# The last, half-empty contraction block of a SwiGLU down projection, run as pairs of 64-row matmuls

## The chip, the cores and the metric

The kernel runs on one core of one Trainium2 chip. The metric is the device time of one execution in microseconds (us). The engines are named as the profile names them: PE does matmuls, PEld loads their stationary operand, DVE is the vector engine, ACT the scalar engine, POOL the general one, and SP issues nearly all DMAs.

## The reference

One adaLN block on 2048 tokens of width 640: a spectral filter (layer norm, 2-D FFT, a filter, inverse FFT) and a SwiGLU feed-forward, each with scale, shift and gate from a small conditioning vector. Only the feed-forward matters here; its inner width is 1728.

```python
def _B_ref(x, w_gate, w_up, w_down):          # x (1, 2048, 640), F = 1728
    g = _silu(x @ w_gate)
    u = x @ w_up
    return g * u @ w_down
...
sa, ca, ga, sb, cb, gb = (mod[:, 0].copy(), ...)
x = x + ga * _A_ref(h, A_w_r, A_w_i)
h = _layernorm(x, axis=-1) * (1 + cb) + sb
x = x + gb * _B_ref(h, B_w_gate, B_w_up, B_w_down)
```

## The kernel before

The whole program is written out by hand: each engine does its instructions in the order of the source, and the tile framework adds the semaphore waits. The first part (up to about 97 us of the span) is the spectral filter. It ends in the loop over `dinv`, which leaves the new residual `x1` in SBUF.

The feed-forward takes the 2048 tokens in four chunks of 512 (`sc`), and each chunk as four tiles of 128 tokens (`tl`). The inner width 1728 is 13 blocks of 128 and one of 64; `NFC` is 14, and block 13 is the half-full one.

For one chunk PE first computes gate and up of block 13 together (`gu13`, L727: 64 gate columns and 64 up columns side by side in `Wp13`). ACT applies Silu to the gate half and copies the up half. A DMA on SP (`u13b`, L734) brings the up half to partitions 0 to 63, and DVE multiplies the two into `AT[0:64, 13, :]` after block 2 (L746). Then, for each of the 13 full blocks, PE computes `gps` and `ups` (L740, five matmuls of 512 columns each), ACT takes Silu of `gps` (L743), and DVE multiplies into `AT[:, fc, :]` (L744). `AT` is double-buffered over the chunks (`ATa`, `ATb`). Between these steps DVE and SP prepare the layer norm of the next chunk: `ln2_stats`, `ln2_newton`, `ln2_xn`, the DMA transpose `ln2_turn` (L649), and `ln2_affine` on DVE and ACT.

The down projection (L767 to L777) follows. For each token tile and each half of the 640 outputs (`oa`, `ob`), 14 matmuls of 320 columns accumulate over the blocks: stationary `AT[:, fc, tok]`, moving `Wd_sb[:, fc, half]`. Block 13 is done like the others with 128 rows: rows 64 to 127 of it are zeros in `AT` (L718) and in `Wd_sb` (L600), set once by POOL. DVE adds the residual out of PSUM (L776), and SP stores the tile (L777).

`Wd_sb` arrives by two DMAs (L599 for 13 blocks, L601 for the 64 rows of the last), ahead of `Wu` (L607) and `wm_gb` (L609) in SP's queue. In chunk 0, DVE multiplies the gate `gb` into the 14 blocks of `Wd_sb` (L753), a few after each block of the loop (`folds`); blocks 11, 12 and 13 come after the last.

PSUM is full: the tags `va`, `vb`, `oa` and `ob` have two buffers each. `gu13` and `gps` take `va`, `ups` takes `vb`, and the down projection takes `oa` and `ob`.

Earlier in the program there are a few matmuls on a part of the array: L369 (one row), L536 (one column) and the transpose in `gate_turn` (L256, five columns).

Of the kernel before, what the change touches and what calls it, by code (L numbers as in the profile page):

```python
# [10 lines left out]
F32 = mybir.dt.float32  # L11
BF16 = mybir.dt.bfloat16
ACT = mybir.ActivationFunctionType
ALU = mybir.AluOpType
AX = mybir.AxisListType

S, D, FF = 2048, 640, 1728
NT, P = 16, 128
# [6 lines left out]
NFC = 14  # L25
# [110 lines left out]
def adaln_block_kernel(  # L136
# [12 lines left out]
    nc = tc.nc  # L149
# [8 lines left out]
    out_v = out.rearrange("o (p t) d -> p (o t) d", t=NT)  # L158
# [13 lines left out]
    g_bc = [const.tile([P, D], BF16, name=n) for n in ("ga_bc", "gb_bc")]  # L172
# [254 lines left out]
    with tc.tile_pool(name="ph2", bufs=2) as ph2, \  # L427
# [122 lines left out]
        for it in range(NU + 2):  # L550
            if it == 0:
                PPs[0] = [product(0, h, X) for h, X in enumerate(Xs.pop(0))]
            if it + 1 < NU:
                Xs[it + 1] = stage_a(it + 1)
            if it + 2 < NPE:
                t2(it + 2)
            if it == 0:
                mod_shat(0, 128)
            if 0 < it < NU:
                X = Xs.pop(it)  # L560
                PPs[it] = [product(it, 0, X[0])]
            if 0 <= it - 1 < NU:
                PP = PPs.pop(it - 1)
                Y2s[it - 1] = []
                for h in range(len(PP)):
                    yps = stage_b(it - 1, h, PP[h])
                    Y2s[it - 1].append(evict_y(it - 1, h, yps))
            if 0 < it < NU and len(X) > 1:
                PPs[it].append(product(it, 1, X[1]))
            if it == 1:  # L570
                m_ps = ps2.tile([P, 2, NC5], F32, name="m_ps", tag="eps_", bufs=2)
                mod_cols(m_ps[:, 0], wm_g, 0)
                mod_cols(m_ps[:, 1], wm_g, 1)
                nc.scalar.copy(g_col[0][:], m_ps[:, 0])
                nc.scalar.copy(modcols[:, 3, :], m_ps[:, 1])
                nc.scalar.add(one_p_cb[:], m_ps[:, 1], 1.0)
                gate_turn(ps2, "eps_", 2, 0)
                nc.sync.dma_start(wm_sb[:], wm_v[:, :, 3 * D:4 * D])
                nc.sync.dma_start(Rinv_sb[:], Rinv_dram)
                gate_spread(0)  # L580
            if 0 <= it - 2 < NU:
                stage_c(it - 2, Y2s.pop(it - 2))
            if 4 <= it < 8:
                epx(it - 4)
            if it in (8, 9):
                nc.vector.tensor_tensor(Rinv_sb[:, it - 8], Rinv_sb[:, it - 8],
                                        g_bc[0][:, it - 8::2].unsqueeze(1).to_broadcast([P, 3, 320]), ALU.mult)
            if it == 5:
                transposed(6)
                transposed(7)  # L590
                nc.sync.dma_start(Htab[:], H_dram)
            if it == 6:
                Wg = big.tile([P, NC5, FFM], BF16, name="Wg", tag="wg")
                nc.sync.dma_start(Wg[:], B_w_gate[:, 0:FFM].rearrange("(c5 dp) f -> dp c5 f", dp=P))
                for i, w_ in enumerate((B_w_gate, B_w_up)):
                    nc.sync.dma_start(Wp13[:, :, 64 * i:64 * i + 64], w_[:, FFM:FF].rearrange("(c5 dp) f -> dp c5 f", dp=P))  # L596
            if it == 8:
                Wd_sb = big.tile([P, NFC, D], BF16, name="Wd_sb", tag="b21a")
                nc.sync.dma_start(Wd_sb[:, 0:13, :], B_w_down[0:FFM, :].rearrange("(fc fp) d -> fp fc d", fp=P))  # L599
                nc.gpsimd.memset(Wd_sb[64:128, 13, :], 0.0)  # L600
                nc.sync.dma_start(Wd_sb[0:64, 13, :], B_w_down[FFM:FF, :])  # L601
            if it == NU + 1:
                m_ps = ps2.tile([P, NC5], F32, name="m_ps", tag="xps", bufs=2)
                mod_cols(m_ps, wm_sb, 0)
                nc.scalar.copy(modcols[:, 2, :], m_ps[:])
                Wu = big.tile([P, NC5, FFM], BF16, name="Wu", tag="wu")
                nc.sync.dma_start(Wu[:], B_w_up[:, 0:FFM].rearrange("(c5 dp) f -> dp c5 f", dp=P))  # L607
                wm_gb = big.tile([P, NC5, D], BF16, name="wm_gb", tag="wb")
                nc.sync.dma_start(wm_gb[:], wm_v[:, :, 5 * D:6 * D])  # L609
# [4 lines left out]
    x1 = x_sb  # L614
# [38 lines left out]
    def ln2_affine(sc, c5s):  # L653
        h2T = h2T_all[:, sc % 2]
        for c5 in c5s:
            if c5 % 2 == 0:
                nc.vector.tensor_scalar(h2T[:, :, c5, :], h2T[:, :, c5, :], one_p_cb[:, c5:c5 + 1], modcols[:, 2, c5:c5 + 1],
                                        ALU.mult, ALU.add)
            else:
                nc.scalar.activation(h2T[:, :, c5, :], h2T[:, :, c5, :], ACT.Identity,  # L660
                                     scale=one_p_cb[:, c5:c5 + 1], bias=modcols[:, 2, c5:c5 + 1])
# [52 lines left out]
    mod_cols(mg_ps, wm_gb, 0)  # L714
    nc.scalar.copy(g_col[1][:], mg_ps[:])
    AT2 = [big.tile([P, NFC, 512], BF16, name=n, tag=g) for n, g in (("ATa", "wb"), ("ATb", "b35"))]
    for a in AT2:
        nc.gpsimd.memset(a[64:128, 13, :], 0.0)  # L718
    nc.scalar.activation(warm[:], rstd2[:, 3:4], ACT.Silu)

    folds = {5: (0,), 6: (1,), 7: (2,), 8: (3, 4), 9: (5, 6), 10: (7, 8), 11: (9, 10), 12: (11, 12, 13)}
    for sc in range(4):
        h2T = h2T_all[:, sc % 2]
        AT = AT2[sc % 2]
        gu13 = ps3.tile([P, 512], F32, name="gu13", tag="va")
        for c5 in range(NC5):
            nc.tensor.matmul(gu13[:], lhsT=Wp13[:, c5, :], rhs=h2T[:, :, c5, :],  # L727
                             start=(c5 == 0), stop=(c5 == NC5 - 1))
        sg13 = ph4.tile([64, 512], F32, name="sg13", bufs=1)
        nc.scalar.activation(sg13[:], gu13[0:64, :], ACT.Silu)  # L730
        u13 = ph4.tile([P, 512], BF16, name="u13", bufs=1)
        nc.scalar.copy(u13[64:128, :], gu13[64:128, :])
        u13b = ph4.tile([64, 512], BF16, name="u13b", bufs=1)
        nc.sync.dma_start(u13b[:], u13[64:128, :])  # L734
        for fc in range(NFC - 1):
            gps = ps3.tile([P, 512], F32, name="gps", tag="va")
            ups = ps3.tile([P, 512], F32, name="ups", tag="vb")
            for w_, o in ((Wg, gps), (Wu, ups)):
                for c5 in range(NC5):
                    nc.tensor.matmul(o[:], lhsT=w_[:, c5, fc * 128:(fc + 1) * 128], rhs=h2T[:, :, c5, :],  # L740
                                     start=(c5 == 0), stop=(c5 == NC5 - 1))
            sg = ph4.tile([P, 512], F32, name="sg", bufs=2)
            nc.scalar.activation(sg[:], gps[:], ACT.Silu)  # L743
            nc.vector.tensor_tensor(AT[:, fc, :], ups[:], sg[:], ALU.mult)  # L744
            if fc == 2:
                nc.vector.tensor_tensor(AT[0:64, 13, :], u13b[:], sg13[:], ALU.mult)  # L746
            if sc == 0:
                if fc == 0:
                    gate_turn(ps3, "oa", 2, 1)
                    gate_spread(1)  # L750
                for f in folds.get(fc, ()):
                    n = P if f < 13 else 64
                    nc.vector.tensor_tensor(Wd_sb[0:n, f, :], Wd_sb[0:n, f, :], g_bc[1][0:n, :], ALU.mult)  # L753
            if sc < 3:
                n0 = 4 * (sc + 1)
                if fc in (1, 2, 3, 4):
                    ln2_stats(n0 + fc - 1)
                if fc == 5:
                    ln2_newton(sc + 1)
                if fc in (6, 7):  # L760
                    ln2_xn(n0 + 2 * (fc - 6))
                    ln2_xn(n0 + 2 * (fc - 6) + 1)
                if fc == 7:
                    ln2_turn(sc + 1)
        if sc < 3:
            ln2_affine(sc + 1, range(NC5))
        for tl in range(4):  # L767
            t = 4 * sc + tl
            tok = slice(tl * 128, (tl + 1) * 128)
            xo = ph4.tile([P, D], BF16, name="xo", bufs=3)  # L770
            os_ = [ps3.tile([P, 320], F32, name=n) for n in ("oa", "ob")]
            for h in range(2):
                for fc in range(NFC):
                    nc.tensor.matmul(os_[h][:], lhsT=AT[:, fc, tok], rhs=Wd_sb[:, fc, h * 320:(h + 1) * 320],  # L774
                                     start=(fc == 0), stop=(fc == NFC - 1))
                nc.vector.tensor_tensor(xo[:, h * 320:(h + 1) * 320], os_[h][:], x1[:, t, h * 320:(h + 1) * 320], ALU.add)  # L776
            nc.sync.dma_start(out_v[:, t, :], xo[:])  # L777


@with_exitstack  # L780
# [45 lines left out]
```

## Time and profile before

| what | us |
|---|---|
| median of 3 runs | 281.56 (280.31 to 281.94) |
| the profiled execution: span, first to last instruction | 279.0 |
| the profiled execution: whole time | not given beside its span; the median lies 2.56 above it |
| PE busy in the span | 268.6 (96%) |
| DVE busy | 163.6 (59%) |
| ACT busy | 112.8 (40%) |
| matmuls of gate and up, L740 (520) | 129.2 |
| matmuls of the down projection, L774 (448) | 66.3 |
| DVE adds of the output, L776 (32) | 15.7 |

The page shows one execution. Busy time of PE adds up the stretches in which at least one matmul is in flight; the mean length of a matmul (299 ns for 320 columns) is longer than its step in a stream, since neighbours overlap. Weight loads (PEld) run beside matmuls. A line of the timeline gives the start, the length, the engine, the source line, the operation with output and inputs, its tile (rows*columns), the moving shape, the count, and in brackets how long the engine stood idle before it and for whom. The granted clock is full in every slice.

### The profile page before, as it was taken

The numbers are of one execution on the slowest core, as the hardware profiler recorded it, in microseconds if no ns is written. First come the engines' busy times: TensorE is split into PE (matmuls) and PEld (weight loads), VectorE is DVE, ScalarE is ACT, GpSimd is POOL, SyncE is SP. The second block draws the span as 40 slices with busy tenths as digits, with TensorE's granted clock in tenths as the row PEclk, the third lists the DMA queues.
The fourth block names the chain that finished last, engine by engine and source line by source line (L and its number), as shares of the span: only waits on it lengthen the run. The fifth ranks groups of instructions, "written<-read, shape, count | busy, mean of one in ns | idle before, by whom it ended". The sixth has DMA issues, their size and how long they took to land.

```text
span 279.0 us, 5262 instructions
## 1 busy us (share of the span) xinstructions
PE 268.6 (96%) x2120; PEld 170.3 (61%) x2120; DVE 163.6 (59%) x411; ACT 112.8 (40%) x220; POOL 10.5 (4%) x34
## 2 busy tenths in 40 slices
PE   6899979999899999999999999999999999999995
PEld 6567768998787844446754445764444774444673
DVE  4999966799499738876227845224872422422322
ACT  5998666998455663222022323003233103223000
POOL 1000023312000010000000000000000000000000
PEclk9999999999999999999999999999999999999999
DMA  7989999999994100050110050101013011000011
GB/s 263 411 220 209 349 324 183 220 307 366 356 363 77 29 27 6 0 96 0 49 56 3 0 96 0 47 26 33 0 33 63 25 47 35 1 0 2 0 47 47
DMA packets 40634, 30.82 MB, mean 110 GB/s; under 512 B 29281, under 2 KB 37410, under 8 KB 40482
## 3 DMA queue, kind: packets, MB, share of 16 engines
q1 hardware_dynamic: 40608, 30.49, 38.3%
q8 instruction: 16, 0.26, 0.4%
q14 instruction: 8, 0.07, 0.1%
q10 hardware_dynamic: 2, 0.00, 0.0%
HBM read 22.88 MB, written 3.93 MB: 96 GB/s over the span
## 4 chain that ended last, share of the span: by engine, by line
PE 74%; DMA 10%; SPq 9%; DVE 4%; ACT 1%; issue 1%; ACTq 0%; DVEq 0%
PE gps L740 20%; PE ups L740 20%; PE ob L774 11%; PE oa L774 10%; DMA Wd_sb<-in_B_w_down_dram 4%; SPq L218 4%; DMA wm_sa<-in_w_mod_dram 3%; DMA Gtab<-tab_G 2%; PE oa L689 2%; SPq L596 2%; PE gu L727 2%; PE ob L689 1%; DVE x_sb L692 1%; SPq L223 1%; PE yps L488 1%; PE xps L463 1%
## 5 line engine op out<-in xcount | busy, mean ns | idle before, releaser
L740 PE MATMUL gps<-h2T_all,Wg 128*128 128x512 bf16 x260 | 64.6, 379 | 0.0
L740 PE MATMUL ups<-h2T_all,Wu 128*128 128x512 bf16 x260 | 64.6, 379 | 0.0
L743 ACT ACTIVATE sg<-gps 128x512 f32<-128x512 f32 x52 | 31.0, 597 | 74.0 <-PE gps L740 72.3
L740 PEld LDWEIGHTS <-Wu 128*128 128x128 bf16 x260 | 25.5, 98 | 30.6
L740 PEld LDWEIGHTS <-Wg 128*128 128x128 bf16 x260 | 25.4, 98 | 30.5
L744 DVE TENSOR_TENSOR ATb<-ups,sg 128x512 bf16<-128x512 f32 x26 | 17.9, 690 | 32.0 <-PE ups L740 32.0
L744 DVE TENSOR_TENSOR ATa<-ups,sg 128x512 bf16<-128x512 f32 x26 | 17.9, 687 | 20.4 <-PE ups L740 17.5
L774 PEld LDWEIGHTS <-ATa 128*128 128x128 bf16 x224 | 21.9, 98 | 9.3 <-issue 0.5
L774 PEld LDWEIGHTS <-ATb 128*128 128x128 bf16 x224 | 21.9, 98 | 8.8
L730 ACT ACTIVATE sg<-gu 64x512 f32<-64x512 f32 x4 | 2.3, 586 | 46.6 <-PE gu L727 46.6
L776 DVE TENSOR_TENSOR xo<-ob,x_sb 128x320 bf16<-128x320 f32 x16 | 7.9, 492 | 22.1 <-PE ob L774 22.1
L776 DVE TENSOR_TENSOR xo<-oa,x_sb 128x320 bf16<-128x320 f32 x16 | 7.8, 491 | 18.4 <-PE oa L774 18.4
L774 PE MATMUL oa<-Wd_sb,ATa 128*128 128x320 bf16 x112 | 16.8, 299 | 0.1
L774 PE MATMUL oa<-Wd_sb,ATb 128*128 128x320 bf16 x112 | 16.5, 299 | 0.0
L774 PE MATMUL ob<-Wd_sb,ATb 128*128 128x320 bf16 x112 | 16.5, 299 | 0.0
L774 PE MATMUL ob<-Wd_sb,ATa 128*128 128x320 bf16 x112 | 16.5, 299 | 0.0
L309 PE MATMUL zps<-Rs,hT 128*128 128x328 bf16 x90 | 14.7, 303 | 0.1
L280 DVE BATCH_NORM_STATS2 st<-x_sb 128x6 f32<-128x320 bf16 x32 | 13.8, 470 | 0.8 <-DMA x_sb<-in_A_x_dram 0.8
L681 ACT CAST VT<-va 128x512 bf16<-128x512 f32 x16 | 9.4, 586 | 8.0 <-PE va L677 6.2
L488 PE MATMUL yps<-identb,PP 128*128 128x128 bf16 x162 | 11.5, 219 | 0.6 <-DVE PP L479 0.4
L466 ACT CAST X<-xps 128x512 bf16<-128x512 f32 (+1 forms) x21 | 11.2, 598 | 1.6 <-PE xps L464 1.6
L309 PEld LDWEIGHTS <-hT 128*128 128x128 bf16 x96 | 8.8, 98 | 4.8 <-ACT hT L305 0.8
(204 smaller groups left out, 407.0 us busy)
## 6 DMA issues: line engine op xcount, KB each, us to landing
out_dram<-xo SPq DMA_DIRECT2D x16, 160.0 KB, 1.8
Wg<-in_B_w_gate_dram SPq DMA_DIRECT2D x1, 2080.0 KB, 12.8
Wd_sb<-in_B_w_down_dram SPq DMA_DIRECT2D x1, 2080.0 KB, 13.4
Wu<-in_B_w_up_dram SPq DMA_DIRECT2D x1, 2080.0 KB, 9.7
x_sb<-in_A_x_dram SPq DMA_DIRECT2D x3, 640.0 KB, 9.3
wm_g<-in_w_mod_dram SPq DMA_DIRECT2D x2, 800.0 KB
Gtab<-tab_G SPq DMA_DIRECT2D x4, 384.0 KB, 8.2
Htab<-tab_H SPq DMA_DIRECT2D x1, 1536.0 KB, 7.1
```

Of the source, the lines that this page charges most:

```text
L218: nc.sync.dma_start(to[0:15, 0], wv[1:16, 0])
L280: nc.vector.bn_stats(sts[t][:, h, :], x_sb[:, t, 320 * h:320 * h + 320])
L309: nc.tensor.matmul(zap, lhsT=hTs[t][:, 2 * r + i, :], rhs=Rs[:, 3 * r + i, :], start=(i == 0), stop=(i == 2))
L466: nc.scalar.copy(X[:, :n].rearrange("p i c k j -> p i (c k j)"), xps[:, :n, :])
L488: nc.tensor.matmul(yps[:, i, :], lhsT=PP[:, i, cp].rearrange("p a k j -> p (a k j)"), rhs=identb[:], start=(cp == 0), stop=(cp == 1))
L681: nc.scalar.copy(VTs[t][:, 0:4, :], va[:])
L689: nc.tensor.matmul(os_[odd][:], lhsT=VT[:, 2 * odd + ci if ci < 2 else 4, :], rhs=Rinv_sb[:, odd, ci, :], start=(ci == 0), stop=(ci == 2))
L740: nc.tensor.matmul(o[:], lhsT=w_[:, c5, fc * 128:(fc + 1) * 128], rhs=h2T[:, :, c5, :], start=(c5 == 0), stop=(c5 == NC5 - 1))
L743: nc.scalar.activation(sg[:], gps[:], ACT.Silu)
L744: nc.vector.tensor_tensor(AT[:, fc, :], ups[:], sg[:], ALU.mult)
L774: nc.tensor.matmul(os_[h][:], lhsT=AT[:, fc, tok], rhs=Wd_sb[:, fc, h * 320:(h + 1) * 320], start=(fc == 0), stop=(fc == NFC - 1))
L776: nc.vector.tensor_tensor(xo[:, h * 320:(h + 1) * 320], os_[h][:], x1[:, t, h * 320:(h + 1) * 320], ALU.add)
```

## The change

Block 13 is no longer padded with zeros. Its 64 rows, of `Wd_sb` and of `AT`, are held twice, on partitions 0 to 63 and 64 to 127. A second DMA brings the weight rows, and a DMA from SBUF to SBUF copies the rows of `AT` in each chunk. The three memsets on POOL go. The fold of the gate into block 13 covers all 128 rows.

For block 13 the output half `h = 0` uses rows 0 to 63 and `h = 1` rows 64 to 127, so that a token tile has a pair of 64-row matmuls in place of two of 128 rows. The eight of a chunk stand together, after the 13 full blocks of the first two tiles and before those of the last two. For the first two tiles they end the accumulation, for the last two they start it. Since all four tiles are then open at once, the last two accumulate in the tags `va` and `vb`. The output adds of the first two tiles come after the group.

```diff
-                nc.gpsimd.memset(Wd_sb[64:128, 13, :], 0.0)
-                nc.sync.dma_start(Wd_sb[0:64, 13, :], B_w_down[FFM:FF, :])
+                for o in (0, 64):
+                    nc.sync.dma_start(Wd_sb[o:o + 64, 13, :], B_w_down[FFM:FF, :])
...
-    for a in AT2:
-        nc.gpsimd.memset(a[64:128, 13, :], 0.0)
...
                 nc.vector.tensor_tensor(AT[0:64, 13, :], u13b[:], sg13[:], ALU.mult)
+                nc.sync.dma_start(AT[64:128, 13, :], AT[0:64, 13, :])
...
-                    n = P if f < 13 else 64
-                    nc.vector.tensor_tensor(Wd_sb[0:n, f, :], Wd_sb[0:n, f, :], g_bc[1][0:n, :], ALU.mult)
+                    nc.vector.tensor_tensor(Wd_sb[:, f, :], Wd_sb[:, f, :], g_bc[1][:], ALU.mult)
...
+        acc = [[ps3.tile([P, 320], F32, name=("oa", "ob")[h], tag=(("oa", "ob"), ("va", "vb"))[tl // 2][h])
+                for h in range(2)] for tl in range(4)]
+
+        def down13(tl, h):
+            r = slice(64 * h, 64 * h + 64)
+            nc.tensor.matmul(acc[tl][h][:], lhsT=AT[r, 13, tl * 128:(tl + 1) * 128],
+                             rhs=Wd_sb[r, 13, h * 320:(h + 1) * 320], start=(tl > 1), stop=(tl < 2))
+
+        def down(tl, h):
+            for fc in range(NFC - 1):
+                nc.tensor.matmul(acc[tl][h][:], lhsT=AT[:, fc, tl * 128:(tl + 1) * 128],
+                                 rhs=Wd_sb[:, fc, h * 320:(h + 1) * 320],
+                                 start=(tl < 2 and fc == 0), stop=(tl > 1 and fc == NFC - 2))
...
+        for tl in range(2):
+            for h in range(2):
+                down(tl, h)
         for tl in range(4):
-            t = 4 * sc + tl
-            tok = slice(tl * 128, (tl + 1) * 128)
-            xo = ph4.tile([P, D], BF16, name="xo", bufs=3)
-            os_ = [ps3.tile([P, 320], F32, name=n) for n in ("oa", "ob")]
             for h in range(2):
-                for fc in range(NFC):
-                    nc.tensor.matmul(os_[h][:], lhsT=AT[:, fc, tok], rhs=Wd_sb[:, fc, h * 320:(h + 1) * 320],
-                                     start=(fc == 0), stop=(fc == NFC - 1))
-                nc.vector.tensor_tensor(xo[:, h * 320:(h + 1) * 320], os_[h][:], x1[:, t, h * 320:(h + 1) * 320], ALU.add)
-            nc.sync.dma_start(out_v[:, t, :], xo[:])
+                down13(tl, h)
+        for tl in range(2):
+            for h in range(2):
+                x_out(tl, h)
+        for tl in range(2, 4):
+            for h in range(2):
+                down(tl, h)
+                x_out(tl, h)
```

`x_out(tl, h)` is the add of the residual for one half, with the store of the tile after the second half.

## The prediction

> **What bounds the kernel now.** I read the page first: busy time, the forty slices, and the chain that ended last.
>
> ```profile
> PE 268.6 (96%) x2120; PEld 170.3 (61%) x2120; DVE 163.6 (59%) x411; ACT 112.8 (40%) x220; POOL 10.5 (4%) x34
> ...
> PE   6899979999899999999999999999999999999995
> ...
> PE 74%; DMA 10%; SPq 9%; DVE 4%; ACT 1%; issue 1%; ACTq 0%; DVEq 0%
> ```
>
> The matmul engine is busy in 96% of the span, and from slice 15 (about 98 us) on every slice shows 9 but the last, which holds the closing add and store. The change lies wholly in that stretch, the feed-forward part. Next I read the chain in order of time around the end of the first chunk.
>
> ```profile
> 137.00 1.90 PE ob L774 x14
> 138.90 1.90 PE oa L774 x14
> 140.80 1.90 PE ob L774 x14
> 142.71 1.08 PE gu L727 x5
> ```
>
> Fourteen matmuls of 320 columns take 1.90 us, so one takes 0.136 us of the stream (the 299 ns that the groups give is latency, and neighbours overlap). The next group starts when the last one ends: nothing but PE sets the time, so every nanosecond of PE stream saved here comes off the end, and every one added goes on it. The one exception is the first chunk:
>
> ```profile
> 126.89 2.51 PE L774 MATMUL oa<-Wd_sb,ATa 128*128 128x320 bf16 x14
> 127.16 0.69 DVE L744 TENSOR_TENSOR ATa<-ups,sg 128x512 bf16<-128x512 f32 x1 [0.67 <-PE ups L740]
> 127.77 1.28 DVE L753 TENSOR_TENSOR Wd_sb<-Wd_sb,gb_bc 128x640 bf16<-128x640 bf16 x3
> 128.70 0.10 PEld L774 LDWEIGHTS <-ATa 128*128 128x128 bf16 x1 [0.22 <-issue]
> ...
> 129.10 0.37 PEld L774 LDWEIGHTS <-ATa 128*128 128x128 bf16 x3 [0.30 <-issue]
> 129.23 0.43 PE L774 MATMUL ob<-Wd_sb,ATa 128*128 128x320 bf16 x2
> ```
>
> The first 14 matmuls need 126.89 to 129.23 = 2.34 us where 1.90 is the rule. Two loads stand waiting, at 128.70 and 129.10: DVE is still folding the gate into weight blocks 11, 12 and 13 (three operations from 127.77 to 129.05).
>
> Last, how PE passes between a full array and a tile of it. The built program marks three kinds of matmul before as partial tiles (32 rows at L369; 32 columns at L536 and L256); here they are in the timeline of PE.
>
> ```profile
> 2.12 0.29 PE L369 MATMUL cps<-one,c_row 1*128 1x1 bf16 x5 [2.12 <-DMA c_row<-in_c_dram]
> 2.35 1.46 PE L267 MATMUL w_ps<-identb 128*128 128x128 bf16 x12
> ...
> 42.89 0.28 PE L446 MATMUL t2ps<-identb,A_sb 128*128 128x128 bf16 x2
> 43.09 0.82 PE L536 MATMUL sps<-Rp,sa_col 128*1 128x256 bf16 x6
> 43.94 0.23 PE L463 MATMUL xps<-Ktab,B 128*128 128x128 bf16 x1
> ...
> 45.07 1.37 PE L243 MATMUL m_ps<-sc_col,wm_g 128*128 128x1 bf16 x49
> ...
> 99.65 1.24 PE L740 MATMUL ups<-h2T_all,Wu 128*128 128x512 bf16 x5
> 100.83 0.22 PE L256 MATMUL gT_ps<-identb,gb_col 128*5 128x128 bf16 x1
> 100.98 1.25 PE L740 MATMUL gps<-h2T_all,Wg 128*128 128x512 bf16 x5
> ```
>
> Into the tile: five ups matmuls at 0.216 end their stream at 100.73, the small tile starts at 100.83: 0.10 us. Out: its 128 columns take 0.055 (the step of neighbouring 128-column matmuls), and the next starts at 100.98: 0.095. Before L536, two steps of 0.055 from 42.89 give 43.00 and the start is 43.09: 0.09. After it, 6 x 0.109 give 43.745 and the start is 43.94: 0.20, but there the load waited for ScalarE too. After L369, the only row tile, five steps of 0.032 give 2.28 and the next starts at 2.35: 0.07. So a switch costs 0.07 to 0.20, and I take 0.095, where the row nearest in place (L256, inside this stage) stands.
>
> **The change, part by part.**
> - *Removed:* 8 of the 112 matmuls of a chunk (the blocks fc = 13 of four tiles by two halves), 8 x 0.136 = 1.088 us.
> - *Added:* 8 matmuls of 64 rows, as four pairs on rows 0 to 63 and 64 to 127. The built program gives the two members different tile positions (0 and 64), and they write different PSUM tiles (oa and ob, or va and vb). If the members run side by side, four pairs take 4 x 0.136 = 0.544, plus a lag of the last member of about 0.03 (one issue: the 49 loads and matmuls at 45.07 need (1.37 - 0.16) / 48 = 0.025 each). No row shows two row tiles at once, so this is bounded: 0.544 if fully parallel, 1.088 if not at all. I take parallel, since the members differ in rows, in PSUM tile and in position, and nothing in the program orders one behind the other.
> - *Two switches per chunk,* 2 x 0.095 = 0.19 (0 to 0.40). So the group takes 0.544 + 0.03 + 0.19 = 0.764 and saves 0.324 per chunk, **1.30 us over four**.
> - The TensorE page of the Trainium skill ("TensorE: Matmul & The Clock Gate", Measured speedup vs the span model) has four row tiles at 3.07 times one, 77% of the full gain. By that share two tiles would give 1.53, the eight matmuls 0.71 and the change in all -1.0 us, 280.5; this is an estimate, and no run here shows it yet.
> - *The stall in the first chunk.* Block 13 is now needed only after both first tiles, 52 matmuls on. Block 12 still holds its matmul to about 128.70; the next would then start at 128.84, not at 129.10. **0.26 us saved, once.** What is late next is nothing on DVE: its affine steps merely follow.
> - *The copy of AT's block 13 to rows 64 to 127* (SP, 64 KB, four times). Its twin u13b takes 0.48 us to issue and lands in 1.9 us. In chunk 0, DVE ends that block at 106.9, so it lands near 109.3; the group comes near 134. It waits on SP for DVE; queued behind it is only the transpose of the next chunk, which itself waits for DVE several steps later (SP waits 18.4 us there). Zero; if the cover went it would cost about 2 us a chunk.
> - *A second copy of the last weight rows* (80 KB) ahead of Wu and wm_gb. The present one took 4.20 us to issue at 66.75, Wu 0.38 at 73.78. If the new one takes 4.2 too, Wu and wm_gb are issued up to 1.3 us later; they land about 83.5 and 85.4 now and are first read at 99.4 and 96.7. Zero, 11 us of cover.
> - *Three POOL memsets* (0.5 to 0.6 us each) go, off the path. The fold of block 13 covers 128 rows instead of 64: 477 to 484 ns for all fourteen, so zero.
> - *Evictions.* Four adds of 0.49 us now come in one burst (2.0 us) beside the 26 matmuls of the third tile (3.5 us). Tiles three and four sit in va and vb, whose last users (the Silu of fc 12 ends 0.6 us after its matmuls) are 7 us past. The next chunk takes the third tile's buffers first; the fourth tile's first half is evicted during its second half (1.77 us). The last add and output DMA stay as they are. Zero.
>
> Sum: -1.30 - 0.26 = -1.56 us. The profiled execution spans 279.0; the median of the runs shown, 281.56, lies 2.56 above it, and the page gives no time of its own for that execution beyond the span. That surround is untouched: span 277.5, time **280.0**.
>
> **Rivals.** A: the forecast. With switches of 0 to 0.20 it gives -2.44 to -0.72, so 279.1 to 280.8.
>
> B: the pairs run side by side, but a load for a row half waits until the matmul in that half has ended. Then three of four pairs expose a load, at most the 0.095 of a switch: 0.764 + 0.285 = 1.05 per chunk, -0.16 - 0.26 = -0.42, 281.1. Against it: at full size loads of 98 ns hide wholly under 0.136 us matmuls on the same rows. The same TensorE page (Part 3, The mechanism) says that a load overlaps matmuls in flight only when the row group differs; by that rule B holds. The 98 ns loads hidden here differ from it, at full size at least.
>
> C: the change does not do what it says: the members run one after the other with loads hidden. 1.088 + 0.19 = 1.278, +0.76 - 0.26 = +0.50, 282.1.
>
> D, slower: one after the other, and in the 64-row mode each load stands exposed. At 0.095 for seven loads the group takes 1.94 us, +3.42 - 0.26 = +3.16, **284.7**. It turns past +1.41 us when a load shows more than 0.033 us, since 4 x (0.19 + 7 x 0.033) - 0.26 = 1.4. For it: no row shows a pair running together, and the only row tiles (L369) step at 0.032 where full ones step at 0.025. Against it: the 32-column tiles of L536 step at 0.109 for 256 columns, loads hidden.
>
> **How the numbers follow.** About 0.5% (1.41 us) is what a measurement of this kernel can tell from no change. A has 0.62: 0.48 beyond that bound, 0.14 short of it (larger switches). B has 0.12 and C 0.08, both within it; D 0.18. So faster 0.48, same 0.34, slower 0.18. The range holds A, B and C: 279.1 to 282.1, each end moved out by 0.3, since the three runs themselves lie 280.31 to 281.94; that is 278.8 to 282.4, and D is left out. A's own range is 279.1 to 280.8.
>
> **What would show it.** In the trace after: the 64-row matmuls of a pair starting within 0.03 us of each other and the next pair 0.136 later (A); a step of up to 0.23 between pairs (B); eight steps of 0.136 (C) or more (D). From the last matmul of the second tile to the first of the third: 0.76 us in A. The first 14-matmul stretch of chunk 0 short by 0.26. The prediction is wrong if this group takes over 1.09 us, or if a new wait of PE shows up at it or at the start of a chunk.

## The result and the profile after

The changed kernel takes 279.06 us in the median of 8 runs (278.70 to 280.41), the kernel before 280.89 in 8 runs beside it. The ratio is 0.9942, with a 95% interval of 0.992 to 0.9964. The profiled execution took 279.14 us, with a span of 277.4; that of before had a span of 279.0.

From the page of the changed kernel, busy time and the chain that ended last:

```profile
PE 267.5 (96%) x2120; PEld 168.3 (61%) x2120; DVE 162.6 (59%) x411; ACT 112.7 (41%) x220; POOL 8.9 (3%) x31
...
PE 86%; DVE 7%; DMA 2%; ACT 2%; issue 1%; SPq 0%; ACTq 0%; DVEq 0%
```

PE is still the bound. Its busy time falls by 1.1 us and the span by 1.6; of the difference, 0.5 lies in the first 40 us, which the edits do not touch (35.7 us busy before, 36.2 now). So the gain is read from starts, first in the chain in order of time. Before:

```profile
97.64 1.10 PE gu L727 x5
...
187.06 1.08 PE gu L727 x5
...
275.80 0.49 DVE xo L776
```

And in the changed kernel:

```profile
97.54 1.10 PE gu L725 x5
...
140.25 1.77 PE ob L775 x13
142.01 1.08 PE gu L725 x5
...
186.03 1.08 PE gu L725 x5
...
274.11 0.49 DVE xo L785
```

From one chunk's `gu13` to the next it is now 186.03 - 142.01 = 44.02 us; before it was 187.06 - 142.71 = 44.35. Each chunk after the first is 0.33 us shorter. The first, from 97.54 here and 97.64 before, has 44.47 in place of 45.07, 0.60 shorter. The timeline of the changed kernel shows both reasons, the start of chunk 0's down projection and its group of pairs:

```profile
126.79 2.11 PE L775 MATMUL oa<-Wd_sb,ATa 128*128 128x320 bf16 x13
127.67 1.28 DVE L751 TENSOR_TENSOR Wd_sb<-Wd_sb,gb_bc 128x640 bf16<-128x640 bf16 x3
128.60 1.05 PEld L775 LDWEIGHTS <-ATa 128*128 128x128 bf16 x8 [0.22 <-issue]
128.74 1.11 PE L775 MATMUL ob<-Wd_sb,ATa 128*128 128x320 bf16 x7
...
132.94 1.25 PE L775 MATMUL ob<-Wd_sb,ATa 128*128 128x320 bf16 x8
134.12 0.39 PEld L770 LDWEIGHTS <-ATa 64*128 64x128 bf16 x8 [0.26 <-issue]
134.13 0.31 PE L770 MATMUL oa<-Wd_sb,ATa 64*128 64x320 bf16 x1
134.13 0.31 PE L770 MATMUL ob<-Wd_sb,ATa 64*128 64x320 bf16 x1
134.27 0.30 PE L770 MATMUL oa<-Wd_sb,ATa 64*128 64x320 bf16 x1
...
134.54 0.30 PE L770 MATMUL oa<-Wd_sb,ATa 64*128 64x320 bf16 x1
...
134.78 0.99 PE L775 MATMUL oa<-Wd_sb,ATa 128*128 128x320 bf16 x6
```

One load waits instead of two: the first 13 matmuls take 128.74 - 126.79 = 1.95 us, 0.18 over their 1.77, where before 14 took 0.44 over 1.90. A stream is taken to end one step (0.136 us) after its last start. The eight full matmuls from 132.94 end their stream at 134.03, and the first pair starts at 134.13, both members within 0.01 us; the next pair follows at 134.27. The last pair starts at 134.54 and ends its stream at 134.68; the full tile goes on at 134.78. The group takes 0.75 us, two switches of 0.10 us included.

On SP, the two weight copies and what was queued behind them:

```profile
68.00 4.09 SPq L601 DMA_DIRECT2D Wd_sb<-in_B_w_down_dram  x2
73.67 0.38 SPq L607 DMA_DIRECT2D Wu<-in_B_w_up_dram  x1
```

Both copies together took 4.09 us to issue, from 68.00 to 72.09, and `Wu` went out at 73.67 (73.78 before).

### The profile page after: what moved, and what is told of

The parts are those of the page before. It is cut to its first block, busy times and chain, and to the rows that moved or that the text cites. A ratio compares the mean times of both kernels' runs of the same rounds, so it can differ in the third digit from the quotient of the medians.

```text
span 277.4 us, 5268 instructions
## 1 busy us (share of the span) xinstructions
PE 267.5 (96%) x2120; PEld 168.3 (61%) x2120; DVE 162.6 (59%) x411; ACT 112.7 (41%) x220; POOL 8.9 (3%) x31
## 4 chain that ended last, share of the span: by engine, by line
PE 86%; DVE 7%; DMA 2%; ACT 2%; issue 1%; SPq 0%; ACTq 0%; DVEq 0%
PE gps L738 20%; PE ups L738 20%; PE oa L775 10%; PE ob L775 10%; PE zps L309 3%; PE yps L488 3%; DMA Rp<-tab_R 2%; PE xps L463 2%; PE oa L689 2%; PE xps L464 2%; PE gu L725 2%; DVE st L280 2%; PE ob L689 1%; DVE x_sb L692 1%; PE t1ps L301 1%; PE aps L332 1%
## 5 line engine op out<-in xcount | busy, mean ns | idle before, releaser
L775 PEld LDWEIGHTS <-ATa 128*128 128x128 bf16 x208 | 20.2, 98 | 8.8 <-issue 0.8
L775 PEld LDWEIGHTS <-ATb 128*128 128x128 bf16 x208 | 20.2, 98 | 8.6 <-issue 0.5
L775 PE MATMUL oa<-Wd_sb,ATa 128*128 128x320 bf16 x104 | 15.6, 299 | 0.0
L775 PE MATMUL oa<-Wd_sb,ATb 128*128 128x320 bf16 x104 | 15.5, 299 | 0.0
L775 PE MATMUL ob<-Wd_sb,ATb 128*128 128x320 bf16 x104 | 15.4, 299 | 0.0
L775 PE MATMUL ob<-Wd_sb,ATa 128*128 128x320 bf16 x104 | 15.4, 299 | 0.0
```

The source lines that it names most:

```text
L775: nc.tensor.matmul(acc[tl][h][:], lhsT=AT[:, fc, tl * 128:(tl + 1) * 128], rhs=Wd_sb[:, fc, h * 320:(h + 1) * 320], start=(tl < 2 and fc = ...
```

## The experiments

The edits leave PE's program in the first 97 us of the span as it is (all but e8's), yet that part moves by about 2 us between profiles. So the spans that the expectations of e1 to e4 give were missed by 0.5 to 1.7 us, and the table has, beside the ratio of times, the stretch that the edits touch: from the first `gu13` to the start of the last output add. It repeats within 0.01 us where one program was profiled twice (second and eighth row). "Group" is from the end of the stream before the 64-row matmuls to the next full matmul, in the second chunk; for the changed kernel it is the one above.

| kernel | ratio to before (95%) | stretch, us | first chunk | second chunk | group |
|---|---|---|---|---|---|
| before | | 178.16 | 45.07 | 44.35 | |
| changed | 0.9942 (0.992 to 0.9964) | 176.57 | 44.47 | 44.02 | 0.75 |
| e1, order only | 0.9991 (0.9968 to 1.0014) | 177.89 | 44.80 | 44.36 | 1.09 |
| e2, same rows | 1.0008 (0.9985 to 1.0031) | 178.74 | 45.02 | 44.56 | 1.28 |
| e3, halves apart | 0.9939 (0.9908 to 0.9971) | 176.61 | 44.48 | 44.03 | 0.76 |
| e4, group per tile | 1.0048 (1.0024 to 1.0073) | 179.43 | 45.01 | 44.66 | 4 x 0.34 |
| e5, copies only | 1.0007 (0.9986 to 1.0029) | 178.17 | 45.08 | 44.35 | |
| e7, change again | 0.9954 (0.993 to 0.9979) | 176.58 | 44.48 | 44.02 | |
| e6, folds earlier | 0.9947 (0.9926 to 0.9968) | 176.39 | 44.29 | 44.02 | |
| e8, folds and PE fed | 0.9943 (0.9919 to 0.9967) | 176.39 | 44.30 | 44.02 | |

**e1, the new order with the padded block.** The zeros come back, the copies go; the group stays where it is.

```diff
...
+    for a in AT2:
+        nc.gpsimd.memset(a[64:128, 13, :], 0.0)
...
-                nc.sync.dma_start(AT[64:128, 13, :], AT[0:64, 13, :])
...
-            r = slice(64 * h, 64 * h + 64)
+            r = slice(0, 128)
```

> Block 13 is again 128 rows with zeros, no copies, but in the new order (all eight matmuls between the second and third tile, last two tiles in va and vb). Theory (the gain is pairs side by side less two switches of 0.1 us, plus 0.26 us of the first chunk's stall): the group takes 8 x 0.136 = 1.09 us with no gap before or after it, the first 13 matmuls of chunk 0 start their successors 1.95 us on as in the changed kernel, the span is 277.4 + 4 x (1.09 - 0.75) = 278.8 us, 0.26 less than the kernel before; ratio to before 0.999. Rival (the new order alone makes the gain): span 277.4, ratio 0.994.

The timeline of e1 at the group of the second chunk, its first matmul and the full one behind it:

```profile
179.69 0.30 PE L772 MATMUL oa<-Wd_sb,ATb 128*128 128x320 bf16 x1
...
180.78 0.43 PE L777 MATMUL oa<-Wd_sb,ATb 128*128 128x320 bf16 x2
```

Eight steps of 0.136 with no gap: 1.09 us. The stretch is 0.27 shorter than before, all of it in the first chunk. So the order takes away the part of the stall that the fold of block 13 made, and does nothing else; the ratio cannot tell that from no change. The span missed (280.0, not 278.8) because the feed-forward began 1.3 us later in that profile.

**e2, both members on the same rows.**

```diff
-            r = slice(64 * h, 64 * h + 64)
+            r = slice(0, 64)
```

> The changed kernel, but both members of a pair use rows 0 to 63. Theory (members run side by side because they lie on different row halves, and loads are hidden even for the same half): eight matmuls start 0.136 us apart, the group takes 1.09 + 0.20 = 1.29 us, span 277.4 + 4 x 0.54 = 279.6, ratio to before 1.002. Rival 1 (a load for a half waits for the matmul in it): steps of up to 0.23, group up to 1.95 us, span up to 282.2, ratio up to 1.011. Rival 2 (64-row matmuls overlap whatever the rows): group 0.75, span 277.4, ratio 0.994.

The timeline of e2, the first two matmuls of the group, its last and the full one behind it:

```profile
179.28 0.31 PE L770 MATMUL oa<-Wd_sb,ATb 64*128 64x320 bf16 x1
179.43 0.30 PE L770 MATMUL ob<-Wd_sb,ATb 64*128 64x320 bf16 x1
...
180.25 0.30 PE L770 MATMUL ob<-Wd_sb,ATb 64*128 64x320 bf16 x1
180.47 0.72 PE L775 MATMUL oa<-Wd_sb,ATb 128*128 128x320 bf16 x4
```

They go one after the other: the eight starts of the group run from 179.28 to 180.25, 0.139 a step, and the group takes 1.28 us. The stretch is 2.17 longer than the changed kernel's (2.16 expected). The saving is thus the running side by side on different row halves. A load for a half in use shows no time beyond 0.003 us a step, which rules out the first rival here.

**e3, all of the lower half first, then all of the upper.**

```diff
-        for tl in range(4):
-            for h in range(2):
+        for h in range(2):
+            for tl in range(4):
                 down13(tl, h)
```

> The changed kernel, but in the group all four matmuls of rows 0 to 63 come first, then all four of rows 64 to 127. Theory (PE starts matmuls in program order, so only neighbours on different halves overlap): one overlap, the fourth with the fifth; 7 x 0.136 + 0.20 = 1.15 us for the group, span 277.4 + 4 x 0.40 = 279.0, ratio to before 1.000. Rival (PE takes a matmul of the free half ahead of its turn): group 0.75, span 277.4, ratio 0.994.

The timeline of e3, the first three starts and the full matmul behind the group:

```profile
177.68 0.31 PE L770 MATMUL oa<-Wd_sb,ATb 64*128 64x320 bf16 x1
177.69 0.31 PE L770 MATMUL ob<-Wd_sb,ATb 64*128 64x320 bf16 x1
177.82 0.30 PE L770 MATMUL oa<-Wd_sb,ATb 64*128 64x320 bf16 x1
...
178.34 1.94 PE L775 MATMUL oa<-Wd_sb,ATb 128*128 128x320 bf16 x13
```

The rival was right, and my theory of the order fell. The `ob` matmul is the fifth of the group in the program and starts 0.01 us after the first, ahead of the second, third and fourth. The group takes 0.76 us, 0.01 more than with neighbours paired. The TensorE page of the Trainium skill ("TensorE: Matmul & The Clock Gate", Part 3, The mechanism) has matmuls start and end in strict program order; these starts contradict that for two row halves.

**e4, a pair at the end of each tile.**

```diff
...
-        for tl in range(2):
+        for tl in range(4):
             for h in range(2):
                 down(tl, h)
-        for tl in range(4):
             for h in range(2):
                 down13(tl, h)
-        for tl in range(2):
             for h in range(2):
-                x_out(tl, h)
-        for tl in range(2, 4):
-            for h in range(2):
-                down(tl, h)
                 x_out(tl, h)
```

In every tile the 13 full matmuls now start the accumulation and the pair ends it.

> The changed kernel, but each tile has its pair at its own end: four groups of one pair per chunk, eight switches instead of two, all else alike. Theory (a switch between full and 64-row tiles costs 0.10 us wherever it stands): a tile's pair takes 0.136 + 0.20 = 0.34 us, 1.35 per chunk against 0.75, span 277.4 + 4 x 0.60 = 279.8, ratio to before 1.003. Rival (the 0.10 is the start of the first loads after a semaphore wait, which only the first pair of a chunk has, not the switch): about 0.14 to 0.20 per tile, span 277.0 to 277.6, ratio 0.994.

The timeline of e4 around the first pair of the second chunk, the start of the second, and the last two adds of the kernel (the first from the chain):

```profile
174.67 1.93 PE L775 MATMUL ob<-Wd_sb,ATb 128*128 128x320 bf16 x13
176.53 0.31 PE L770 MATMUL oa<-Wd_sb,ATb 64*128 64x320 bf16 x1
...
176.77 1.94 PE L775 MATMUL oa<-Wd_sb,ATb 128*128 128x320 bf16 x13
...
180.41 0.31 PE L770 MATMUL oa<-Wd_sb,ATb 64*128 64x320 bf16 x1
...
277.84 0.48 DVE xo L785
278.24 0.48 DVE L785 TENSOR_TENSOR xo<-ob,x_sb 128x320 bf16<-128x320 f32 x1
```

The stream before ends at 176.44, the pair starts 0.09 later, and the full tile 0.10 after the pair's stream. Each tile pays 0.34 us. The stretch is 2.86 longer than the changed kernel's: 2.46 (2.4 expected) are 24 more switches at 0.10, and 0.40 come at the end, which the expectation left out, since both adds of the last tile now wait for its pair. The second pair starts 3.88 us after the first, two streams of 1.77 and 0.34 more, so it pays as much as the first; the rival, by which only the first pair of a chunk would, falls. Pairs placed like this make the kernel slower than before, 1.0048: a pair saves 0.136 and its two switches cost 0.20.

**e5, the data movement alone**, on the kernel before.

```diff
-                nc.gpsimd.memset(Wd_sb[64:128, 13, :], 0.0)
-                nc.sync.dma_start(Wd_sb[0:64, 13, :], B_w_down[FFM:FF, :])
+                for o in (0, 64):
+                    nc.sync.dma_start(Wd_sb[o:o + 64, 13, :], B_w_down[FFM:FF, :])
...
+                at13 = ph4.tile([P, 512], BF16, name="at13", bufs=2)
+                nc.sync.dma_start(at13[64:128, :], AT[0:64, 13, :])
...
-                    n = P if f < 13 else 64
-                    nc.vector.tensor_tensor(Wd_sb[0:n, f, :], Wd_sb[0:n, f, :], g_bc[1][0:n, :], ALU.mult)
+                    nc.vector.tensor_tensor(Wd_sb[:, f, :], Wd_sb[:, f, :], g_bc[1][:], ALU.mult)
```

> The kernel before with the change's data movement alone: the last 64 weight rows brought twice (in place of the memset of Wd_sb), the fold of block 13 over 128 rows, and block 13 of AT copied by SP in each chunk, to a tile that nothing reads. Theory (the copies and the wider fold are covered): from one chunk's gu13 to the next 44.35 us as before, first down-projection stretch of chunk 0 2.34 us, ratio to before 1.000. Rival (the copies hold SP or the transfers of Wu, wm_gb or the next chunk's transpose): a wait of PE at a chunk's start or in the first chunk, a longer chunk, ratio over 1.001.

The stretch is 178.17 against 178.16, both chunks within 0.01. The copies and the wider fold cost nothing that shows in the stretch; the ratio alone, 0.9986 to 1.0029, would not tell the rival from the theory.

**e6 and e7, the folds earlier, and the change once more.**

```diff
-    folds = {5: (0,), 6: (1,), 7: (2,), 8: (3, 4), 9: (5, 6), 10: (7, 8), 11: (9, 10), 12: (11, 12, 13)}
+    folds = {5: (0,), 6: (1,), 7: (2,), 8: (3, 4), 9: (5, 6, 7), 10: (8, 9, 10), 11: (11, 12), 12: (13,)}
```

> The changed kernel with the gate folds of weight blocks 7 to 13 spread one step earlier (three after blocks 9 and 10, two after 11, one after 12, in place of two, two, two and three). Theory (what is left of chunk 0's stall, 0.18 us, is PE waiting for the fold of block 12): the first half of the first tile takes 13 x 0.136 = 1.77 us instead of 1.95, the chunk before its second gu13 44.30 instead of 44.47, ratio to before 0.993 to 0.994. Rival (PE waits for the multiply of block 12, not the fold, or DVE with three folds in a step is late for the next multiply): 1.95 stays or a wait moves into the gate and up matmuls, ratio as the changed kernel or worse.

> The changed kernel once more, beside the two others on the same chip: group 0.75 us, chunk 44.03 us, first chunk 44.47, ratio to before 0.994 by the theory (four chunks of 0.33 and 0.26 once, of 281). Rival (part of the measured 1.6 us came from the first 97 us, which move by about 1 us from run to run): ratio nearer to 0.997.

The timeline of e6, first tile of the first chunk:

```profile
126.93 1.93 PE L775 MATMUL oa<-Wd_sb,ATa 128*128 128x320 bf16 x13
...
128.69 1.93 PE L775 MATMUL ob<-Wd_sb,ATa 128*128 128x320 bf16 x13
```

The first 13 matmuls now take 1.76 us: the stall is gone, and the first chunk is 0.18 to 0.19 shorter than in e7 or the changed kernel. So what was left of it was a fold. The trace of the changed kernel tells which: the second of its three folds from 127.67, that of block 12, ends near 128.55, and the matmul of block 12, the 13th, starts at 128.74 - 0.136 = 128.60. This version has the shortest stretch. In times the 0.07% cannot be resolved: 0.9947 and 0.9954 have overlapping intervals. The change measured again is at 0.9954. That interval holds the 0.994 of e7's theory and the 0.997 of its rival alike; the stretch decides: it is 176.58 again, 1.58 us under before, whatever the first 97 us do.

**e8, folds earlier and PE fed during a wait.** The folds of e6, and ten 128-column matmuls whose result nothing uses, ahead of the 25 that wait for `wm_sa`.

```diff
         go(plan)
+        keep_warm(ps1, "t1ps", 2, 10)
         mod_sa()
```

> The changed kernel with the folds spread earlier, and ten 128-column matmuls of no use on PE ahead of the 25 one-column matmuls that wait for wm_sa (near 37 us). In three of the profiles PE's granted clock was halved for 3.4 us after that wait, and the feed-forward began at 98.8 to 99.2 us; in the others it began at 97.1 to 98.9. Theory (the wait and the one-column matmuls leave PE too idle, and the halved stretch costs about 1.6 us where it comes): no profile and no run below clock 0.997, spread narrower, median about 0.4 us under that of the earlier folds alone, ratio to before 0.992 to 0.994. Rival (the clock is granted by something that ten short matmuls do not change, or they only delay the 25): runs at clock 0.994 as often as before, ratio 0.995 or more.

Inconclusive. The median is 279.23 us where e6 had 279.82, 0.59 less (0.4 expected), but on another chip. One of 12 runs still had the lower clock (4 of 12 in e6 and in e7), and the ratio does not part from theirs. "No run" was wrong; "less often" is not shown with such numbers.

## Why the prediction was right

**The pairs.** Forecast 0.544 + 0.03 us for the eight; from the first start, 134.13, to the end of the last stream, 134.68, it is 0.55. They run side by side (e2 shows 1.28 for the group when they cannot). The lag of 0.03 was too large, 0.01 at most. No row before showed two row tiles at once, so that they would overlap was a bet, argued and put at 0.62, and it came out. The prediction also took a share of 77% of the full gain from the Trainium skill ("TensorE: Matmul & The Clock Gate", Measured speedup vs the span model), where it is that of four row tiles; by that estimate the eight would have taken 0.71. Here two tiles give the full factor of two, 1.09 against 0.55.

**The switches.** 0.095 us, taken over from a row of a column tile; 0.09 to 0.10 at the 64-row tiles. The only row tile before, L369, had shown 0.07, so that the number fits this well is in part luck. The Trainium skill's page "TensorEngine Tiling (Array Packing)" (Key Properties) says that a change of tiling mode drains the engine and gives no time. The trace has a gap at every switch, which fits. That it is a drain is not shown: the last full matmul, by its modelled end (132.94 + 1.25 = 134.19), is still in flight when the pair starts at 134.13, and the first 64-row load starts only at 134.12, so the gap may also be the wait of that load.

**The group and the chunk.** 0.764 forecast, 0.75 measured; 0.324 a chunk forecast, 0.33 measured.

**The stall in chunk 0.** 0.26 forecast; 0.44 fell to 0.18, which is 0.26, and e1 alone brings 0.27. The rest is the fold of block 12 (e6), as the step had it.

**The sum.** -1.56 forecast; the stretch went from 178.16 to 176.57, -1.59, and the span from 279.0 to 277.4 (277.5 forecast). The median came out at 279.06 and not 280.0, just under the forecast's own 279.1 to 280.8, because the term from span to time was wrong: 2.56 us was the median of three runs less the span of another execution. Every run whose span is on record lies 1.7 to 1.9 us above it (279.14 against 277.4 here); with 1.75 the forecast span of 277.44 gives 279.2. The three runs also lay high: the median of before, taken with the result, is 280.89. Beside it the medians differ by 1.83 us; the ratio, 0.9942, stands for 1.63.

**The terms put at zero.** The copies: e5. The second weight copy could have put `Wu` 1.3 us later and did not: both were issued in 4.09 us, about the 4.20 that one had taken, and SP then stood idle for 1.58 us before `Wu` (2.83 before), so `Wu` went out when something else released it. The evictions: the next chunk's `gu13` starts where the last stream ends (140.25 + 1.77 = 142.02, start 142.01), so no wait took the place of what went.

**The rivals.** C does not hold: the pairs overlap. B and D both needed loads to stand exposed in the 64-row mode; e2, where every load is for the half in use, steps at 0.139. The rule by which the prediction let B hold is therefore not borne out for these loads, and the measurement decides. If C had come true it would have looked like e2, 0.58 us over before, against the 0.50 worked out. The step "nothing in the program orders one behind the other" was right for a stronger reason than I had: PE does not even keep the order of the program between the halves (e3).

## What to carry to other kernels

A half-empty contraction block is worth two 64-row matmuls side by side only where the two switches are shared: a pair of 320 columns saves 0.136 us, a visit to the 64-row mode costs 0.20, so one pair per visit loses and four gain 0.33. The two members need different row halves (e2), and how the halves are interleaved did not matter over four and four (e3); that they write different PSUM tiles was kept throughout and not varied. Where the gain is a few tenths of a microsecond, compare a stretch of the trace that begins after the parts that vary, and move late preparation (here the folds) off the first use.

## What the runs showed of the hardware that was not expected

Besides the two halves running ahead of each other (e3), part of the noise of this kernel shows in the trace. These are windows of the same two microseconds, first of the kernel before, then of e7; columns: window, length, busy time (and count) of PE, PEld, DVE, ACT and POOL, granted PE clock, DMA share, GB/s.

```profile
40.00:42.00 2.00, 1.24 (x23) 1.07 (x21) 1.39 (x4) 1.56 (x3) 1.32 (x4) 1.00 1.72 187
```

```profile
40.00:42.00 2.00, 1.95 (x22) 1.76 (x19) 1.18 (x3) 1.15 (x3) 0.96 (x2) 0.50 1.86 235
```

In e7 the clock is halved here, for 3.4 us in all; so it is in e4 and e5, and in no other profile between 11 us and the last matmuls. It follows a wait for `wm_sa` and the 25 one-column matmuls after it, here in e7, e4 and e1:

```profile
38.23 0.78 PE L243 MATMUL mpsB<-sc_col,wm_sa 128*128 128x1 bf16 x25 [0.97 <-DMA wm_sa<-in_w_mod_dram]
```

```profile
37.73 0.78 PE L243 MATMUL mpsB<-sc_col,wm_sa 128*128 128x1 bf16 x25 [0.45 <-DMA wm_sa<-in_w_mod_dram]
```

```profile
38.76 0.78 PE L243 MATMUL mpsB<-sc_col,wm_sa 128*128 128x1 bf16 x25 [0.83 <-DMA wm_sa<-in_w_mod_dram]
```

The length of the wait does not decide: 0.45 us in e4 has the halved clock, 0.83 in e1 has not. What fits all ten profiles is a count. The stretches of full clock in the traces are whole multiples of 3.413 us (34.13 is 10 of them, 269.65 is 79). Cut into such pieces from the first full clock on, every piece in which matmuls of at most 2977 moving columns in all start is followed by the half clock, and none with 2994 or more is; the piece that ends near 40 us has 2121 to 2977 in e4, e5 and e7, 3069 before and 3217 in e1. This was found in the traces afterwards, and no run sets it apart (e8 is inconclusive).

The feed-forward began at 99.22 in e7 and 97.54 in the first profile of the same kernel. Of these 1.68 us, 0.77 stand already where the 25 matmuls start (38.23 against 37.46), so the halved clock accounts for about 0.9 and not for the 1.6 that e8 expected.
